# Warm-up, head-wise values and turned blocks in an attention-then-GEGLU kernel on one core

## The chip, the core and the metric

The kernel runs on one core of a Trainium2 chip. The core has five engines that run side by side, each through its own queue in order: TensorE (PE, matmuls and transposes into PSUM; its weight loads are shown as PEld), VectorE (DVE), ScalarE (ACT), GpSimd (POOL) and SyncE (SP). DMAs are issued from the queues of SP and POOL and run on 16 shared DMA engines. [...] The metric is the device time of one execution in microseconds (us), lower is better.

## The reference

Attention over 8 batches of 8 heads, with 16 "beacon" keys and values ahead of 576 causal ones, and then a gated feed-forward block over the 4608 tokens:

```python
B, H, S, D = q.shape                       # 8, 8, 576, 64; Nb = 16
k_all = concat([beacon_k, k], axis=2)      # 592 keys
v_all = concat([beacon_v, v], axis=2)
scores = q @ k_all.T / sqrt(D)
scores = where(causal, -1e9, scores)       # beacons are seen by every query
a = softmax(scores)
x = (a @ v_all).transpose(0, 2, 1, 3).reshape(B * S, H * D)   # 4608 x 512
g = x @ w_gate                             # 512 x 1536
out = (gelu(g) * (x @ w_val)) @ w_out      # 1536 x 512, result 4608 x 512 float32
```

The kernel computes it in bfloat16 with float32 sums.

## The kernel before

**Attention of one batch.** Heads are handled in pairs (`NPAIR` = 4, index m; `hi` is the head within the pair). Queries and keys lie turned in `qkT`. Scores of a pair come out turned (keys on partitions), in four chunks of columns (`CHUNKS`); `scores` (L246) does the matmuls of two or three chunks into one of the three two-bank buffers of the pool `psum_s`, lets ScalarE take the exp into `exp_ring`, and from batch 1 on lets POOL zero the masked part with `affine_select` (`masks`, L292). In batch 0 the mask is added on TensorE from two small constants, `eye` and `neg`. `attend` (L313) multiplies the exps with the values, which carry a column of ones, so that the row sums come along; `normalize` (L341) on VectorE takes the reciprocal and multiplies, into `y_sb`. For a pair both heads lie in one two-bank buffer `x_ps` of `psum_s`; batch 0's first pair alone uses the two one-bank pools `psum_t` and `psum_o`.

**Turning y.** The feed-forward block wants x with the features on partitions, in `xT_sb`. `turn` (L359) does five transposes on TensorE into PSUM and `put` (L378) copies them out; `turn_dma` (L367) does it with DMA transposes from SP. In batches 1 to 7 pairs 0 and 1 go by DMA (three each), pairs 2 and 3 by TensorE.

**Feed-forward.** Tokens go in nine chunks of 512. `gv_mms` (L390) does gate and value matmuls of one slot fi of 128 features (twelve slots, four k-chunks kk, one for each head pair), ScalarE the gelu, VectorE the product into `hT_sb`. `out_mms` (L452) does the output matmuls: 48 for a chunk, four tiles ti of twelve, whose sums lie by turns in `psum_t` and `psum_o`; `out_store` (L442) copies a finished tile and stores it from SP.

**Order.** The order on every engine is that of the program (`keep`). The main loop (L558) runs over the batches b; in it `o(n)` puts the next n output matmuls of chunk b - 1 between the attention steps of batch b, so that TensorE has work while ScalarE takes exps. After the attention come the gate and value matmuls of chunk b. Once the masks of batch b are done, POOL issues the loads of v for batch b + 1 and of q and k for b + 2 (batches 1 to 6 have at least one of these). SP first stores and turns y, then issues ten DMA transposes of the next batch's q and k (`transpose_dma`, L235). Chunk b needs columns 512b to 512b + 511 of `xT_sb`, batch b writes columns 576b to 576b + 575; so chunk 7 needs only the first 64 tokens of batch 7.

**The start.** Before batch 0's data are there, `warm(50)` (L230, L520) keeps TensorE busy with matmuls of the constant `idle`. Queries and keys of batches 0 and 1 are turned on TensorE from `qk` (`transpose_half`, L210; `transpose_pe`, L197). POOL makes `eye` and `neg` (L467 to L489) between its loads.

Of the kernel before, what the change touches and what calls it, by code (L numbers as in the profile page):

```python
# [7 lines left out]
P = 128  # L8
B, H, S, NB, D = 8, 8, 576, 16, 64
SK = S + NB  # L10
N_TOK = B * S
# [40 lines left out]
def kernel(  # L52
# [23 lines left out]
    psum_o = ctx.enter_context(tc.tile_pool(name="psum_o", bufs=1, space=bass.MemoryType.PSUM))  # L76

    eye = const.tile([P, 256], BF16, name="eye", tag="eye")
    nc.vector.memset(eye, 0.0)
    ident = eye[:, 64:192]  # L80
    idle = const.tile([P, P], BF16, name="idle", tag="idle")
    nc.vector.memset(idle, 0.0)
    wg_sb = const.tile([P, K_CHUNKS, D_FF], BF16, name="wg_sb", tag="wg_sb")
    wv_sb = const.tile([P, K_CHUNKS, D_FF], BF16, name="wv_sb", tag="wv_sb")
    wo_sb = const.tile([P, F_TILES, D_MODEL], BF16, name="wo_sb", tag="wo_sb")
    xT_sb = const.tile([P, NPAIR, N_TOK], BF16, name="xT_sb", tag="xT_sb")

    exp_ring = ring.tile([P, NPAIR, 2, EXP_W + P - Q_N[4]], BF16, name="expT", tag="expT")
    nc.vector.memset(exp_ring[:, :, :, EXP_W:], 0.0)
# [13 lines left out]
    nc.vector.memset(qkT[:, :, 1, SK:640], 0.0)  # L103

    neg = const.tile([P, 256], BF16, name="neg", tag="neg")
    nc.vector.memset(neg, 0.0)

    def dma(out_ap, in_ap):
        keep(nc.gpsimd.dma_start(out=out_ap, in_=in_ap))  # L112
# [62 lines left out]
    def mm(out_ap, lhsT, rhs, start, stop, **kw):  # L175
        keep(nc.tensor.matmul(out_ap, lhsT, rhs, start=start, stop=stop, **kw))  # L176
# [33 lines left out]
    def transpose_half(b, m, w, by_act=False):  # L210
        pool, tag = ((psum_o, "o"), (psum_t, "t"))[w]
        t_ps = pool.tile([P, 1024], BF16, name="t_ps", tag=tag)
        tr_part(b, m, w, t_ps)
        out_ap = qkT[:, m, w, NB:SK].rearrange("p (t r) -> p t r", r=6)
        in_ap = t_ps[:, 0:S].rearrange("p (r t) -> p t r", r=6)
        if by_act:
            act(out_ap, in_ap, ACT.Copy)
        else:
            keep(nc.vector.tensor_copy(out_ap, in_ap))  # L219
        return t_ps  # L220
# [9 lines left out]
    def warm(n):  # L230
        w_ps = psum_s.tile([P, 2, 512], FP32, name="w_ps", tag="s")
        for j in range(n):
            mm(w_ps[:, 0, 0:D], idle, idle[:, 0:D], True, True)

    def transpose_dma(b):  # L235
        q_sb, k_sb = q_ring[b % NRING], k_ring[b % NRING]
# [73 lines left out]

    x_of = {}

    def attend(b, m, where="s"):  # L313
        i = b * NPAIR + m
        if where == "ot":
            x_ps = (
                psum_t.tile([P, 512], FP32, name="xt_ps", tag="t"),
                psum_o.tile([P, 512], FP32, name="xo_ps", tag="o"),
            )
            x_of[i] = [(x_ps[hi].rearrange("p (b c) -> p b c", b=1), hi, hi + 1) for hi in range(2)]  # L320
        else:
            x = psum_s.tile([P, 2, 512], FP32, name="x_ps", tag="s")
            x_ps = (x[:, 0, :], x[:, 1, :])
            x_of[i] = [(x, 0, 2)]
        expT, v_sb = exp_ring[:, m, :, :], v_ring[b % NRING]
        for j in range(5):
            for hi in range(2):
                for t in range(j + 1):
                    e0 = EXP_OFF[t] + S_LO[j] - S_LO[t]
                    mm(  # L330
                        x_ps[hi][:, j * DV : (j + 1) * DV],
                        expT[0 : KROWS[t], hi, e0 : e0 + P],
                        v_sb[0 : KROWS[t], t, 2 * m + hi, 0:DV],
                        t == 0,
                        t == j,
                        skip_group_check=True,
                    )

    y_of = {}

    def normalize(b, m):  # L341
        i = b * NPAIR + m
        r_sb = npool.tile([P, 2, 5, 1], FP32, name="r_sb", tag="r_sb")
        y_sb = npool.tile([P, 5, 2, D], BF16, name="y_sb", tag="y_sb")
        y_of[i] = y_sb
        for x_ps, h0, h1 in x_of.pop(i):
            x = x_ps[:, :, 0 : 5 * DV].rearrange("p b (j d) -> p b j d", d=DV)
            r = r_sb[:, h0:h1, :, :]
            keep(nc.vector.reciprocal(r, x[:, :, :, D:DV]))  # L349
            keep(  # L350
                nc.vector.tensor_tensor(  # L351
                    out=y_sb[:, :, h0:h1, :].rearrange("p j b d -> p b j d"),
                    in0=x[:, :, :, 0:D],
                    in1=r.to_broadcast([P, h1 - h0, 5, D]),
                    op=ALU.mult,
                )
            )
# [9 lines left out]
    def turn_dma(b, m):  # L367
        y_sb = y_of.pop(b * NPAIR + m)
        n0 = b * S
        for n, j0, j1, q0 in ((S_LO[1], 0, 1, 0), (P, 1, 4, S_LO[1]), (Q_N[4], 4, 5, S_LO[4])):  # L370
            keep(
                nc.sync.dma_start_transpose(
                    out=xT_sb[:, m, n0 + q0 : n0 + q0 + n * (j1 - j0)].rearrange("p (j n) -> p j n", n=n),
                    in_=y_sb[0:n, j0:j1, :, :].rearrange("p j e d -> p (j e d)"),
                )
            )
# [13 lines left out]
    def gv_mms(ci, fi, *kks, split=False, last=False):  # L390
        if (ci, fi) not in gv_of:
            if split:
                gv_of[ci, fi] = (
                    psum_t.tile([P, CH], FP32, name="g_ps", tag="t"),
                    psum_s.tile([P, 2, CH], FP32, name="v_ps", tag="s")[:, 0, :],
                )
            else:
                gv_ps = psum_s.tile([P, 2, CH], FP32, name="gv_ps", tag="s")
                gv_of[ci, fi] = (gv_ps[:, 0, :], gv_ps[:, 1, :])
        n0 = ci * CH  # L400

        def part(w):
            for kk in kks:
                mm(
                    gv_of[ci, fi][w],
                    (wg_sb, wv_sb)[w][:, kk, fi * P : (fi + 1) * P],
                    xT_sb[:, kk, n0 : n0 + CH],
                    kk == 0,
                    kk == K_CHUNKS - 1,
                    skip_group_check=True,  # L410
                )
# [40 lines left out]
    def out_mms(ci, u0, u1):  # L452
        for u in range(u0, u1):
# [8 lines left out]

    kb_sb = opool.tile([NB, H, D], FP32, name="kb_sb", tag="o_sb")
    keep(nc.sync.dma_start(out=kb_sb, in_=beacon_k[0].rearrange("h t d -> t h d")))
    load_qk6(0, 0, 2)
    load_qk6(0, 2, 4, (1,))
    keep(  # L467
# [8 lines left out]
        )  # L476
    )
    load_qk6(0, 2, 4, (0,))
    keep(
        nc.gpsimd.affine_select(  # L480
            out=neg,
            in_=neg,
            pattern=[[1, 256]],
            compare_op=ALU.is_ge,
            fill=MASKED,
            base=-64,
            channel_multiplier=-1,
        )
    )  # L489
    load_qk6(0, 4, 6)  # L490
    load_qk6(0, 6, H)
    load_v(0)
    load_gate_val(0, 2)
    load_gate_val(2, 4)
    load_gate_val(4, 8)
# [13 lines left out]

    ahead(5)  # L510

    def av(b, m, where="s"):
        attend(b, m, where)
        normalize(b, m)

    def c(*parts):
        scores(0, *parts)

    keep(nc.scalar.preload_act_table_set(SET_EXP))
    warm(50)  # L520
    keep(nc.vector.tensor_copy(qk6[0][1], kb_sb))
    transpose_both(0, 0)
    c((0, 0))
    c((0, 2))
# [10 lines left out]
    c((2, 1))  # L535
    c((3, 0))
    c((3, 2))
    c((2, 3), (3, 3))
    av(0, 0, "ot")
    c((3, 1))  # L540
    av(0, 1)
    av(0, 2)
    turn(0, 0)
    put(0, 0, by_act=True)
# [13 lines left out]
    for b in range(B):  # L558
# [6 lines left out]
        if b:  # L565
# [2 lines left out]
            scores(b, (0, 0))  # L568
            scores(b, (0, 2))
            scores(b, (0, 1))  # L570
            if b == 1:
                transpose_pe(1, 3)
            ahead(2)
            o(9)
            scores(b, (0, 3), (1, 3))
            scores(b, (1, 0))
            scores(b, (1, 2))
            ahead(2)
            o(5)
# [82 lines left out]
```

## Time and profile before

| | |
|---|---|
| median of 8 runs | 372.0 us (371.04 to 372.75) |
| the profiled execution | 372.75 us; span on the core 370.7 us |
| TensorE busy | 358.9 us, 97% of the span |
| ScalarE, VectorE, GpSimd busy | 188.4, 149.6, 160.3 us |
| DMA | 38.33 MB, mean 103 GB/s |

The span runs from the first to the last instruction; the 2.05 us between it and the execution's time lie around it. Instructions are shown with their start in us from the span's beginning, their duration, engine, line of the kernel, operation, out<-in and how many are merged in the row; in brackets is the idle time of the engine before them and what ended it. [...] five output matmuls that begin at 290.99 are followed by other work at 292.08, 0.216 us each. "DMA to landing" is the time from a DMA's issue to its data's arrival, and "PSUM bank" or "buffer" below always means one that an engine still reads when TensorE wants to write it.

### The profile page before, as it was taken

How to read it: one execution, taken by the hardware profiler on the slowest of the kernel's cores; microseconds unless marked ns; L12 is line 12 of the kernel's file. 1: busy time of each engine (PE TensorE's matmuls, PEld its weight loads, DVE VectorE, ACT ScalarE, POOL GpSimd, SP SyncE). 2: the span in 40 equal slices, each digit the busy share in tenths (PEclk: the TensorE clock that was granted, in tenths of full speed). 3: DMA queues.
4: the chain of work that ended last, by engine and by line, in shares of the span. 5: the costliest groups of instructions: out<-in, count | busy, mean ns of one | idle time of the engine just before them, and what ended most of it. 6: DMA issues, size and time to landing. Idle time of an engine off the chain costs nothing.

```text
span 370.7 us, 7504 instructions
## 1 busy us (share of the span) xinstructions
PE 358.9 (97%) x3022; PEld 184.0 (50%) x3072; DVE 149.6 (40%) x254; ACT 188.4 (51%) x243; POOL 160.3 (43%) x284
## 2 busy tenths in 40 slices
PE   7999999999999999999999999999999999999996
PEld 6674545544554455444554455445544554444443
DVE  2454543543344425433444335333444254334332
ACT  3773477436753486338833774357534863331210
POOL 8934377942387146743495149524800430000000
PEclk9999999999999999999999999999999999999999
DMA  7999999999169943999299929991691030000112
GB/s 102 168 198 205 195 117 122 141 124 142 46 123 147 136 53 91 129 152 102 62 143 153 90 73 112 149 135 47 122 148 31 33 94 21 0 2 28 57 39 105
DMA packets 149858, 38.33 MB, mean 103 GB/s; under 512 B 136384, under 2 KB 145344, under 8 KB 149824
## 3 DMA queue, kind: packets, MB, share of 16 engines
q0 software_dynamic: 104992, 19.13, 70.6%
q1 hardware_dynamic: 44832, 18.73, 27.6%
q8 instruction: 24, 0.39, 0.5%
q14 instruction: 10, 0.08, 0.1%
HBM read 38.27 MB, written 9.44 MB: 129 GB/s over the span
## 4 chain that ended last, share of the span: by engine, by line
PE 81%; DMA 10%; POOL 2%; issue 2%; ACT 2%; SPq 1%; DVE 1%; POOLq 0%; ACTq 0%
PE gv_ps L176 36%; PE o_ps L176 24%; PE s_ps L176 8%; PE x_ps L176 7%; DMA q_sb<-in_q_dram 6%; DMA qkT<-k_sb 4%; POOL v_sb L112 2%; PE t_ps L184 2%; ACT expT L179 2%; PE y_ps L184 1%; SPq L240 1%; PE v_ps L176 1%; PE g_ps L176 1%; DMA qk<-in_k_dram 1%; DVE qkT L219 0%
## 5 line engine op out<-in xcount | busy, mean ns | idle before, releaser
L179 ACT ACTIVATE ge_sb<-gv_ps 128x512 bf16<-128x512 f32 x101 | 59.4, 597 | 132.8 <-PE gv_ps L176 132.8
L179 ACT ACTIVATE expT<-s_ps 128x960 bf16<-128x960 f32 (+3 forms) x112 | 100.0, 964 | 22.6 <-PE s_ps L176 21.6
L425 DVE TENSOR_TENSOR hT_sb<-gv_ps,ge_sb 128x512 bf16<-128x512 f32 x101 | 69.1, 691 | 104.9 <-ACT ge_sb L179 104.9
L176 PE MATMUL gv_ps<-xT_sb,wg_sb 128*128 128x512 bf16 x400 | 107.8, 379 | 0.2
L176 PE MATMUL gv_ps<-xT_sb,wv_sb 128*128 128x512 bf16 x390 | 104.1, 379 | 0.4
L176 PE MATMUL o_ps<-wo_sb,hT_sb 128*128 128x512 bf16 (+2 forms) x413 | 100.7, 373 | 2.4 <-issue 1.1
L300 POOL TENSOR_SCALAR_AFFINE_SELECT expT<-expT 128x256 bf16<-128x256 bf16 (+2 forms) x140 | 51.8, 384 | 95.4 <-ACT expT L179 94.4
L176 PEld LDWEIGHTS <-wv_sb 128*128 128x128 bf16 x432 | 42.2, 98 | 50.7
L176 PEld LDWEIGHTS <-wg_sb 128*128 128x128 bf16 x432 | 41.1, 98 | 46.7
L176 PEld LDWEIGHTS <-hT_sb 128*128 128x128 bf16 x444 | 38.9, 98 | 43.8 <-issue 6.3
L444 DVE COPY o_sb<-o_ps 128x512 f32<-128x512 f32 (+2 forms) x37 | 25.0, 676 | 43.4 <-PE o_ps L176 43.3
L176 PE MATMUL s_ps<-qkT 64*128 64x512 bf16 (+5 forms) x384 | 34.1, 291 | 2.6 <-DMA qkT<-k_sb 0.8
L112 POOL DMA_DIRECT2D v_sb<-in_v_dram x40 | 33.6, 862 | 5.9 <-DMA wv_sb<-in_moe_w_val_dram 1.9
L176 PEld LDWEIGHTS <-expT 128*128 128x128 bf16 (+1 forms) x960 | 32.5, 97 | 6.7 <-POOL expT L300 1.6
L112 POOL DMA_DIRECT2D k_sb<-in_k_dram x30 | 25.2, 841 | 20.0 <-DMA q_sb<-in_q_dram 13.2
L176 PE MATMUL x_ps<-v_sb,expT 128*128 128x65 bf16 x930 | 33.3, 194 | 0.0
L112 POOL DMA_DIRECT2D q_sb<-in_q_dram x30 | 25.4, 879 | 6.5 <-DMA wo_sb<-in_moe_w_out_dram 3.5
L351 DVE TENSOR_TENSOR y_sb<-x_ps,r_sb 128x640 bf16<-128x640 f32 x31 | 25.6, 825 | 1.1
L176 PEld LDWEIGHTS <-qkT 64*128 64x128 bf16 x384 | 14.4, 96 | 22.9 <-issue 15.5
L349 DVE RECIPROCAL r_sb<-x_ps 128x10 f32<-128x10 f32 x31 | 6.8, 221 | 36.9 <-PE x_ps L176 36.9
L384 DVE COPY xT_sb<-y_ps 128x576 bf16<-128x576 bf16 x15 | 6.9, 458 | 10.5 <-PE y_ps L184 10.5
L184 PE MATMUL t_ps<-eye,qk 96*64 96x96 bf16 x192 | 8.3, 244 | 1.3 <-ACT expT L179 0.7
(51 smaller groups left out, 127.0 us busy)
## 6 DMA issues: line engine op xcount, KB each, us to landing
out_dram<-o_sb SPq DMA_DIRECT2D x35, 256.0 KB, 2.3
v_sb<-in_v_dram POOLq DMA_DIRECT2D x24, 128.0 KB, 7.6
q_sb<-in_q_dram POOLq DMA_DIRECT2D x24, 128.0 KB, 10.8
k_sb<-in_k_dram POOLq DMA_DIRECT2D x18, 128.0 KB, 9.8
wo_sb<-in_moe_w_out_dram POOLq DMA_DIRECT2D x3, 512.0 KB, 14.1
wg_sb<-in_moe_w_gate_dram POOLq DMA_DIRECT2D x2, 512.0 KB, 11.4
wv_sb<-in_moe_w_val_dram POOLq DMA_DIRECT2D x2, 512.0 KB, 12.9
v_sb<-in_v_dram POOLq DMA_DIRECT2D x8, 112.0 KB, 4.9
```

Of the source, the lines that this page charges most:

```text
L112: keep(nc.gpsimd.dma_start(out=out_ap, in_=in_ap))
L176: keep(nc.tensor.matmul(out_ap, lhsT, rhs, start=start, stop=stop, **kw))
L179: keep(nc.scalar.activation(out_ap, in_ap, func, **kw))
L184: keep(nc.tensor.transpose(out_ap, in_ap, ident[0:n, 0:n]))
L240: nc.sync.dma_start_transpose(out=qkT[:, :, w, c + j * P : c + j * P + n], in_=src[0:n, j, :, :].rearrange("p h d -> p (h d)"),)
L300: nc.gpsimd.affine_select(out=d, in_=d, pattern=[[0, 2], [1, n]], compare_op=ALU.is_ge, fill=0.0, base=NB if t == 0 else 0, channel_multip ...
L349: keep(nc.vector.reciprocal(r, x[:, :, :, D:DV]))
L351: nc.vector.tensor_tensor(out=y_sb[:, :, h0:h1, :].rearrange("p j b d -> p b j d"), in0=x[:, :, :, 0:D], in1=r.to_broadcast([P, h1 - h0, 5 ...
L384: keep(nc.vector.tensor_copy(out_ap, y_ps[:, 0:S]))
L425: nc.vector.tensor_tensor(out=h_of[ci][:, fi, :], in0=gv_of.pop((ci, fi))[1], in1=ge_sb, op=ALU.mult)
L444: keep(nc.vector.tensor_copy(o_sb[:, ti, c0:c1], o_ps))
```

## The change

The start:
- `idle` is widened and set first, 66 warm-up matmuls take the place of 50, and eight transposes of `idle` into an unused part of the PSUM tile are put before the turn of q of batch 0's first pair.
- batch 0's beacon values come over SP's queue as float32 and are cast by VectorE, instead of over POOL's queue.
- `neg` is made on VectorE, by a running sum along the row of `eye` (started at -1) and a scaling, instead of a `memset` and a select on POOL.
- in batch 0 the score chunk ((2, 3), (3, 3)) moves behind the values of pair 0, and (3, 1) behind those of pair 1.

The loop:
- in batch 1, five output matmuls stand before the TensorE turn of pair 3's q and k, four after it.
- pairs 0 and 1 of batches 1 to 7 take their values one head at a time (`av_head`), each into a one-bank tile, pair 0 in `psum_t` and pair 1 in `psum_o`, with scores or output matmuls between the heads.
- pair 2 is turned by DMA instead of by TensorE and a copy. All DMA turns use two transposes for a pair: the last block is taken as a full one, whose 48 extra columns lie in the next batch's place (`xT_sb` is made wider for the last batch).
- output matmuls are put elsewhere: 30 instead of 40 before the last scores, and 18 (6, 7, 5) instead of 8 (6, 2) after them; pair 3 is turned between the 7 and the 5.
- the k-chunks of the first two feature slots come in the order 0, 3, 1, 2, both slots in turn; before it was 0, 1, 2 of slot 0, then 0, 1, 2 of slot 1, then 3 of each, with the turn of pair 3 in between.

```diff
-    idle = const.tile([P, P], BF16, name="idle", tag="idle")
-    xT_sb = const.tile([P, NPAIR, N_TOK], BF16, name="xT_sb", tag="xT_sb")
+    idle = const.tile([P, 256], BF16, name="idle", tag="idle")
+    xT_sb = const.tile([P, NPAIR, N_TOK + P - Q_N[4]], BF16, name="xT_sb", tag="xT_sb")
...
         t_ps = pool.tile([P, 1024], BF16, name="t_ps", tag=tag)
+        for _ in range(8 if by_act else 0):
+            tr(t_ps[0:D, 640:768], idle[:, 0:D])
         tr_part(b, m, w, t_ps)
...
+    def av(b, m):
+        x = psum_s.tile([P, 2, 512], FP32, name="x_ps", tag="s")
+        for hi in range(2):
+            attend(b, m, hi, x[:, hi, :])
+        normalize(b, m, x, 0, 2)
+
+    def av_head(b, m, hi, pool, tag):
+        x = pool.tile([P, 1, 512], FP32, name="x_ps", tag=tag)
+        attend(b, m, hi, x[:, 0, :])
+        normalize(b, m, x, hi, hi + 1)
...
-        for n, j0, j1, q0 in ((S_LO[1], 0, 1, 0), (P, 1, 4, S_LO[1]), (Q_N[4], 4, 5, S_LO[4])):
+        for n, j0, j1, q0 in ((S_LO[1], 0, 1, 0), (P, 1, 5, S_LO[1])):
...
+    vb_sb = opool.tile([NB, H, D], FP32, name="vb_sb", tag="o_sb")
+    keep(nc.sync.dma_start(out=vb_sb, in_=beacon_v[0].rearrange("h t d -> t h d")))
...
-    load_v(0)
+    for load in key_loads(v, beacon_v, v_ring[0][:, :, :, 0:D], 0)[1:]:
+        load()
...
-    warm(50)
+    warm(66)
     keep(nc.vector.tensor_copy(qk6[0][1], kb_sb))
+    keep(nc.vector.tensor_copy(v_ring[0][0:NB, 0, :, 0:D], vb_sb))
+    keep(nc.vector.tensor_tensor_scan(neg, eye, idle, -1.0, ALU.add, ALU.add))
+    keep(nc.vector.tensor_scalar_mul(neg, neg, -MASKED))
...
+    av_head(0, 0, 0, psum_t, "t")
+    av_head(0, 0, 1, psum_o, "o")
     c((2, 3), (3, 3))
-    av(0, 0, "ot")
+    av(0, 1)
     c((3, 1))
-    av(0, 1)
     av(0, 2)
...
+            o(5)
             if b == 1:
                 transpose_pe(1, 3)
             ahead(2)
-            o(9)
+            o(4)
             scores(b, (0, 3), (1, 3))
             scores(b, (1, 0))
             scores(b, (1, 2))
             ahead(2)
-            o(5)
-            av(b, 0)
-            turn_dma(b, 0)
-            o(4)
+            o(6)
+            av_head(b, 0, 0, psum_t, "t")
             scores(b, (1, 1))
             scores(b, (2, 0))
             scores(b, (2, 2))
             ahead(2)
+            o(1)
+            av_head(b, 0, 1, psum_t, "t")
+            turn_dma(b, 0)
             o(5)
-            av(b, 1)
-            turn_dma(b, 1)
-            o(4)
             scores(b, (2, 1))
             scores(b, (2, 3), (3, 3))
             scores(b, (3, 0))
-            o(9)
+            av_head(b, 1, 0, psum_o, "o")
+            o(5)
+            av_head(b, 1, 1, psum_o, "o")
+            turn_dma(b, 1)
             scores(b, (3, 1))
             scores(b, (3, 2))
             av(b, 2)
+            turn_dma(b, 2)
             o(6)
-            turn(b, 2)
-            put(b, 2)
-            o(2)
             av(b, 3)
-            keep(nc.scalar.preload_act_table_set(SET_GELU))
-            gv_mms(b, 0, 0, 1, 2)
-            gv_mms(b, 1, 0)
+            o(7)
             turn(b, 3)
             put(b, 3)
-            gv_mms(b, 1, 1, 2)
-            gv_mms(b, 0, 3, last=True)
-            gv_mms(b, 1, 3, last=True)
+            o(5)
+            keep(nc.scalar.preload_act_table_set(SET_GELU))
+            for kk in (0, 3, 1, 2):
+                for fi in range(2):
+                    gv_mms(b, fi, kk, last=kk == 2)
```

More of the change, by code (lines that the diff above doesn't have):

```diff
@@ L78 @@
     eye = const.tile([P, 256], BF16, name="eye", tag="eye")
+    idle = const.tile([P, 256], BF16, name="idle", tag="idle")
+    nc.vector.memset(idle, 0.0)
     nc.vector.memset(eye, 0.0)
     ident = eye[:, 64:192]
-    idle = const.tile([P, P], BF16, name="idle", tag="idle")
-    nc.vector.memset(idle, 0.0)
     wg_sb = const.tile([P, K_CHUNKS, D_FF], BF16, name="wg_sb", tag="wg_sb")
@@ L105 @@
     neg = const.tile([P, 256], BF16, name="neg", tag="neg")
-    nc.vector.memset(neg, 0.0)
     def dma(out_ap, in_ap):
@@ L232, in warm @@
         for j in range(n):
-            mm(w_ps[:, 0, 0:D], idle, idle[:, 0:D], True, True)
+            mm(w_ps[:, 0, 0:D], idle[:, 0:P], idle[:, 0:D], True, True)
     def transpose_dma(b):
@@ L311, with attend @@
     x_of = {}
[L313 to L324, printed above, removed]
+    def attend(b, m, hi, x_ps):
@@ L325, in attend @@
         expT, v_sb = exp_ring[:, m, :, :], v_ring[b % NRING]
         for j in range(5):
[L327 to L337, printed above, removed]
+            for t in range(j + 1):
+                e0 = EXP_OFF[t] + S_LO[j] - S_LO[t]
+                mm(
+                    x_ps[:, j * DV : (j + 1) * DV],
+                    expT[0 : KROWS[t], hi, e0 : e0 + P],
+                    v_sb[0 : KROWS[t], t, 2 * m + hi, 0:DV],
+                    t == 0,
+                    t == j,
+                    skip_group_check=True,
+                )
@@ L339, with normalize @@
     y_of = {}
-    def normalize(b, m):
+    def normalize(b, m, x_ps, h0, h1):
         i = b * NPAIR + m
+        if h0 == 0:
+            y_of[i] = npool.tile([P, 5, 2, D], BF16, name="y_sb", tag="y_sb")
         r_sb = npool.tile([P, 2, 5, 1], FP32, name="r_sb", tag="r_sb")
[L344 to L356, printed above, removed]
-            )
+        x = x_ps[:, :, 0 : 5 * DV].rearrange("p b (j d) -> p b j d", d=DV)
+        r = r_sb[:, h0:h1, :, :]
+        keep(nc.vector.reciprocal(r, x[:, :, :, D:DV]))
+        keep(
+            nc.vector.tensor_tensor(
+                out=y_of[i][:, :, h0:h1, :].rearrange("p j b d -> p b j d"),
+                in0=x[:, :, :, 0:D],
+                in1=r.to_broadcast([P, h1 - h0, 5, D]),
+                op=ALU.mult,
+            )
+        )
@@ L408, in part @@
                     kk == 0,
-                    kk == K_CHUNKS - 1,
+                    last and kk == kks[-1],
                     skip_group_check=True,
@@ L478 @@
     load_qk6(0, 2, 4, (0,))
[L479 to L489, printed above, removed]
     load_qk6(0, 4, 6)
     load_qk6(0, 6, H)
-    load_v(0)
+    for load in key_loads(v, beacon_v, v_ring[0][:, :, :, 0:D], 0)[1:]:
+        load()
     load_gate_val(0, 2)
@@ L510 @@
     ahead(5)
-    def av(b, m, where="s"):
-        attend(b, m, where)
-        normalize(b, m)
     def c(*parts):
```

## The prediction

> **What bounds the kernel now.** I read the page's first and fourth parts, then the windows by batch, the timelines of the start and of one late batch, and the tile views of the DMA transposes. All times are of the profiled execution.
>
> ```profile
> PE 358.9 (97%) x3022; PEld 184.0 (50%) x3072; DVE 149.6 (40%) x254; ACT 188.4 (51%) x243; POOL 160.3 (43%) x284
> ...
> PE 81%; DMA 10%; POOL 2%; issue 2%; ACT 2%; SPq 1%; DVE 1%; POOLq 0%; ACTq 0%
> ```
>
> TensorE is busy nearly always and is 81% of the chain of waits. Only three things can help: fewer TensorE instructions, a faster TensorE, fewer of its few gaps. The windows, one batch each (window, length, PE busy, clock, DMA share, GB/s), show how small the gaps are:
>
> ```profile
> 88.87:128.94 40.07, 39.12 (x318) 1.00 1.22 114
> 128.94:168.43 39.49, 39.06 (x318) 1.00 1.30 109
> 168.43:208.02 39.59, 38.84 (x317) 1.00 1.18 115
> 208.02:247.32 39.30, 38.87 (x317) 1.00 1.19 112
> ```
>
> A batch without gaps takes 39.30. With the first batch of the loop (47.00 to 87.15: 40.15), the batches' excess over 39.30 is 0.85 + 0.77 + 0.19 + 0.29 = 2.1 us. Two of its causes, from the timelines of PE (start, duration, what, idle before):
>
> ```profile
> 50.61 0.70 PE L184 MATMUL t_ps<-eye,qk 96*64 96x96 bf16 x24 [0.71 <-ACT expT L179]
> ...
> 91.11 0.21 PE L176 MATMUL s_ps<-qkT 64*128 64x80 bf16 x2 [0.52 <-DMA qkT<-k_sb]
> ```
>
> The first is a PSUM buffer that an exp still holds, the second the last transpose of the next batch's keys. The start is different:
>
> ```profile
> 4.59 0.69 PE L184 MATMUL t_ps<-eye,qk 96*64 96x96 bf16 x12 [0.54 <-DMA qk<-in_k_dram]
> ...
> 6.83 0.61 PE L176 MATMUL s_ps<-qkT 64*128 64x512 bf16 x2 [0.74 <-ACT qkT L179]
> ...
> 15.06 0.69 PE L184 MATMUL t_ps<-eye,qk 96*64 96x96 bf16 x12
> ...
> 37.02 0.70 PE L184 MATMUL t_ps<-eye,qk 96*64 96x96 bf16 x24
> ```
>
> 12 transposes take as long at 15.06 as 24 at 37.02: until about 16 us TensorE runs at half speed, though the page's clock row shows 9 everywhere. The 50 warm-up matmuls (1.20 to 4.05) are followed by 0.54 idle, the first scores by 0.74.
>
> [...] neither 2.85 us of warm-up nor the broken stretch after it released it, the unbroken one from 10.46 did. [...] a transpose alone lands 2.4 us after its issue, beside the loads 6 to 10. [...] No scan is in this trace.
>
> **The change, part by part.**
>
> *Start.* 66 warm-up matmuls at 2.69/50 = 0.054 us end at 1.1 + 3.55 = 4.65, where the keys have landed (4.59). Eight transposes of idle data fill the time before q's transposes: at half speed 128 columns cost 12/9 of 96 columns' 0.057, some 0.08 to 0.11 each, 0.85 in all. The unbroken stretch becomes 1.1 to 7.0, 5.9 us[...]. If the clock rises at 5 to 7 us, ScalarE sets the pace instead: first exp about 7.8 (7.61 now, the fillers delay it), 14 exps of about 0.93 less overlap, one gap of 0.6 for pair 1's turned keys: the last ends at 20.6 instead of 16.86 + 5.18 = 22.04. Values, turns and fills behind it then end about 1.65 earlier (pair 3's turn at about 23.8 instead of 25.43). Bounds: -2.2 to +0.9, the latter when the clock stays low and the fillers only delay. Weights do not bind: wv's columns for the fifth slot land at 28.1 and are wanted at 32.6 now. I take -1.65.
>
> *Mask seed and beacon values.* GpSimd loses the neg select (0.44) and one DMA issue (0.58), so later loads are issued earlier. VectorE gains a cast of 16x512 (0.48, the row of kb), a scan and a scaling. [...] Started at 4.0 after the eye, they end by 4.9, before VectorE's key copy (now 5.44). Cost 0 (bound +0.5, if the second beacon transfer lands late).
>
> *Batch 1.* Five output matmuls (1.08) before its turn cover the 0.71: -0.7.
>
> *Turn of pair 2.* It leaves TensorE (303.18 to 303.44 and a gap, 0.30 a batch) and becomes two DMA transposes; pairs 0 and 1 go from three to two each, so SP issues six either way.
>
> *Values one head at a time.* A head is 15 matmuls, 0.455; its bank is freed by one reciprocal and one product:
>
> ```profile
> 20.14 0.20 DVE L349 RECIPROCAL r_sb<-xt_ps 128x5 f32<-128x5 f32 x1 [2.74 <-PE xt_ps L176]
> ...
> 20.37 0.49 DVE L351 TENSOR_TENSOR y_sb<-xt_ps,r_sb 128x320 bf16<-128x320 f32 x1
> ```
>
> That is about 1.0 us after its last matmul. I laid batch 6 (first output matmul 286.47 = 0) out anew, with its timeline's durations: output matmuls of 0.216, score groups of 0.74, 0.79, 0.73, 0.71 and 0.51, each with 0.1 before it. First group 0.96 to 1.70, nine output matmuls, second group 3.73 to 4.53, six, head 0 to 6.29, third group 6.39 to 7.19, one, head 1 to 7.88, five to 9.06, fourth group 9.16 to 9.96, head, five, head to 11.98, fifth group 12.08 to 12.59, pair 2 to 13.5, six to 14.8, pair 3 to 15.75, seven to 17.25, turn to 17.55, five to 18.65, four times four gate/value matmuls to 22.1 (22.04 now). Waits are in it. The third tile of outputs wants bank t 0.89 after head 1 ends: waits 0.1. Scores now come closer together, and with three buffers the last of the third group waits 0.07, of the fourth 0.09. Sum of waits 0.26, against 0.30 saved: -0.02 a batch, -0.15 over seven. Bounds -0.3 to +0.3 each.
>
> *The third pair's DMA.* In that layout the scores of (3,1), (3,2) start at 12.1 (13.9 now). ScalarE, hardly idle since 1.45, does their two exps from 12.5 to 14.3; the mask ends at 14.8, and there GpSimd's queue begins the next loads, as now:
>
> ```profile
> 105.76 0.41 POOL L300 TENSOR_SCALAR_AFFINE_SELECT expT<-expT 128x256 bf16<-128x256 bf16 x1 [0.15 <-ACT expT L179]
> 106.11 0.54 POOL L112 DMA_DIRECT2D v_sb<-in_beacon_v_dram  x1
> 106.65 4.19 POOL L112 DMA_DIRECT2D v_sb<-in_v_dram  x5
> ```
>
> Loads of v thus from 15.3. SP: pair 1's y is ready at 12.9; its two transposes (1.1 and 1.25) and pair 2's first end at 16.55, so pair 2's large one is issued at 16.6, 1.3 after the loads began. TensorE needs it after 12 more output matmuls and 12 gate/value matmuls, at 21.3, that is 4.7 after issue. Alone:
>
> ```profile
> DMA to landing us min/median/max: 2.2/2.4/5.4
> ```
>
> and there is no wait. Beside the loads the nearest rows are the next batch's first transpose (same size, issued 1.6 after the loads began; 6.0 at 108.23, 6.0 to 7.8 in the six loaded batches) and the store just ahead of it (1.1 after, 3.1 to 4.7). The transpose of 108.23 had that store ahead in its ring and landed 3.0 after it; mine has a small transpose ahead, which should be through. So 4.5 to 6.0; I take 4.95, a wait of 0.25 in batches 1 to 6: +1.5. Batch 7 has no loads.
>
> *The next batch's transposes* queue on SP behind the last store, so they start 20.1 after the batch begins (18.6 to 19.4 now), but the loads they share engines with start 1.7 to 2.5 earlier; they should land by about 40.2, wanted at 40.7. The stalls at 91 and 170 go with the rest of the excess: 2.1 - 0.7 - 0.2 kept = -1.2.
>
> **Sum.** 372.75 (the profiled execution; span 370.7 and 2.05 around it) - 1.65 - 0.7 - 0.15 - 1.2 + 1.5 = 370.55. The median of the runs, 372.0, lies 0.75 under the profiled one, which released its clock late; a start that releases early no longer has that spread, so the sum stands as it is: 370.6, 0.4% under the median.
>
> **Rivals.**
>
> *A, slower: the third pair's transpose is late.* It lands like the qkT ones, store or no store, 5.8 after issue, and TensorE waits 1.1 in six batches: 370.55 + 5.1 = 375.7. For it: every transpose within 2 us of a load's start took 6 or more. Against: each had the store ahead. It decides from a wait of 0.5 a batch, where 2.95 us of savings are used up. At 7.8 after issue it would be 3 us a batch, above 386.
>
> *B: the clock stays low* in the new stretch[...]. Then the fillers cost 0.5 to 0.9 and the start saves nothing: about 372.9. For it: 8.05 to 10.3 was busy too, and released nothing.
>
> *C: one-bank buffers* cost 0.3 a batch more (each wait followed by an exposed weight load of 0.1): 372.7.
>
> *D: no wait for the transposes at all:* 369.0.
>
> **How the numbers follow.** Forecast 0.42, A 0.22, B 0.18, C 0.10, D 0.08. About 0.2% (0.75 us) is what a measurement of this kernel can tell from no change. Below 371.25: most of the forecast (0.36), D and a little of B and C (0.03): 0.47. Above 372.75: A, and half of B and C: 0.34. Between: 0.19. The range 368.6 to 376.0 leaves out D's deeper end and A's upper half. The forecast's own range is 369.3 to 371.8.
>
> **What would show it.** Right: 12 transposes in 0.35 us before 10 us; the last exp of batch 0 near 20.6; no gap at batch 1's turn; fill matmuls of the third k-chunk start within 0.5 us of the second's end. Wrong: a gap of about 1 us there, put down to a DMA of y_sb (A); 0.69 for 12 transposes still at 13 us (B); gaps at the head matmuls or the third output tile (C). A batch window much above 39.3 from batch 2 on makes the forecast wrong.

## The result and the profile after

The changed kernel takes 383.66 us (median of 11 runs, 380.44 to 387.77) against 372.45 before: a ratio of 1.027, interval 1.025 to 1.030. Three of the eleven runs (387.4 to 387.8) count as slow, and the ratio leaves them out. The kernel is slower, where 370.6 was forecast. The profiled execution took 381.64, span 379.8.

The page's first and fourth parts for the changed kernel:

```profile
PE 358.0 (94%) x3012; PEld 184.2 (49%) x3061; DVE 152.4 (40%) x277; ACT 188.2 (50%) x243; POOL 159.1 (42%) x282
...
PE 79%; DMA 13%; SPq 3%; DVE 2%; issue 1%; POOL 0%; ACT 0%
```

TensorE has as much to do as before in a longer span: 94% instead of 97%. The new time is idle time. The waits of TensorE's matmuls (who waited <- for what: total us, times, longest) name it:

```profile
PE gv_ps L172 <- DMA xT_sb<-y_sb: 11.0, 7, 2.8
...
PE s_ps L172 <- DMA qkT<-q_sb: 0.6, 1, 0.6
```

The windows of batches 1 to 6, each from its first output matmul to that of the next batch (window, length, busy time of PE, PEld, DVE, ACT, POOL, clock, DMA share, GB/s), show how unequal the batches have become:

```profile
45.94:87.89 41.95, 39.94 (x338) 19.96 (x342) 17.67 (x32) 22.12 (x29) 28.66 (x47) 1.00 1.78 146
87.89:128.66 40.77, 39.07 (x313) 19.65 (x317) 16.26 (x29) 22.13 (x29) 20.96 (x37) 1.00 1.17 109
128.66:171.08 42.42, 39.14 (x312) 19.59 (x317) 16.27 (x29) 22.14 (x29) 20.98 (x37) 1.00 1.16 112
171.08:213.74 42.66, 39.24 (x313) 19.54 (x317) 16.27 (x29) 22.13 (x29) 20.99 (x37) 1.00 1.12 108
213.74:255.15 41.41, 39.06 (x313) 19.64 (x317) 16.26 (x29) 22.13 (x29) 20.99 (x37) 1.00 1.12 110
255.15:295.69 40.54, 39.06 (x313) 19.65 (x317) 16.27 (x29) 22.13 (x29) 12.06 (x26) 1.00 0.56 84
```

A batch without gaps took 39.3 before. What follows the last of these windows takes as long as before (80.94 to the last matmul), so the loss sits in batches 1 to 6. Batch 3 shows the place. GpSimd's timeline, where the next loads begin behind the last mask, and SyncE's, where four transposes (two of pair 1, two of pair 2) stand in one row:

```profile
143.75 0.41 POOL L298 TENSOR_SCALAR_AFFINE_SELECT expT<-expT 128x256 bf16<-128x256 bf16 x1 [0.15 <-ACT expT L175]
144.10 0.53 POOL L108 DMA_DIRECT2D v_sb<-in_beacon_v_dram  x1
144.62 4.20 POOL L108 DMA_DIRECT2D v_sb<-in_v_dram  x5
```

```profile
142.25 5.01 SPq L368 DMA_TRANSPOSE xT_sb<-y_sb  x4
147.35 1.83 SPq L442 DMA_DIRECT2D out_dram<-o_sb  x2
```

and TensorE's:

```profile
150.30 0.38 PE L172 MATMUL gv_ps<-xT_sb,wv_sb 128*128 128x512 bf16 x1
152.94 0.39 PE L172 MATMUL gv_ps<-xT_sb,wg_sb 128*128 128x512 bf16 x1 [2.26 <-DMA xT_sb<-y_sb]
```

The large transpose of pair 2, the last of SyncE's four, is issued at 146.00 and lands at 152.90. The last of TensorE's twelve gate and value matmuls that can do without it begins at 150.30, so the next could begin at 150.52, 0.22 later; it has to wait until 152.94. Each batch issues six transposes of y; the table follows pair 2's large one ("first v load" is the first from `in_v_dram`; the landing without loads is from the second experiment):

| batch | issued after the first v load | landed after issue | same, loads held back | wait |
|---|---|---|---|---|
| 1 | 0.83 | 6.11 | 4.14 | 1.51 |
| 2 | 1.76 | 5.53 | 2.48 | 1.28 |
| 3 | 1.38 | 6.90 | 4.03 | 2.26 |
| 4 | 2.89 | 6.28 | 2.49 | 2.75 |
| 5 | 1.38 | 6.55 | 4.12 | 1.93 |
| 6 | 1.67 | 5.39 | 2.49 | 1.05 |
| 7 | no loads | 3.61 | 3.85 | 0 |

The six waits add up to 10.8. The seventh wait of the 11.0 is 0.24 in batch 4, ahead of k-chunk 1, and belongs to pair 1: its large transpose was issued there at 186.43, beside the loads as well, and landed at 191.77.

The start did what was hoped for:

```profile
4.76 0.69 PE L180 MATMUL t_ps<-eye,qk 96*64 96x96 bf16 x12
...
6.22 0.45 PE L180 MATMUL t_ps<-eye,qk 96*64 96x96 bf16 x12
```

Twelve transposes take 0.69 at 4.76 and 0.45 at 6.22, and the first batch of the loop begins at 45.94 instead of 48.15.

The runs spread over 7 us, and their length goes with the granted clock: those from 380.4 to 382.8 had 0.994 or more, those from 383.7 to 387.8 had 0.986 to 0.990. The profiled one had 1.00. This is taken up in the last experiment.

### The profile page after: what moved, and what is told of

Read it like the earlier page. It is cut to its first block, busy times and chain, and to the rows that moved or that the text cites. A ratio compares the mean times of both kernels' runs of the same rounds, so it can differ in the third digit from the quotient of the medians.

```text
span 379.8 us, 7505 instructions
## 1 busy us (share of the span) xinstructions
PE 358.0 (94%) x3012; PEld 184.2 (49%) x3061; DVE 152.4 (40%) x277; ACT 188.2 (50%) x243; POOL 159.1 (42%) x282
## 4 chain that ended last, share of the span: by engine, by line
PE 79%; DMA 13%; SPq 3%; DVE 2%; issue 1%; POOL 0%; ACT 0%
PE gv_ps L172 38%; PE o_ps L172 20%; DMA xT_sb<-y_sb 9%; PE x_ps L172 8%; PE s_ps L172 8%; DMA qkT<-q_sb 2%; DMA q_sb<-in_q_dram 2%; SPq L238 2%; PE t_ps L180 2%; PE v_ps L172 1%; PE g_ps L172 1%; DVE qkT L217 1%; PE w_ps L172 1%; SPq L368 1%; PE y_ps L180 0%
## 5 line engine op out<-in xcount | busy, mean ns | idle before, releaser
L172 PE MATMUL gv_ps<-xT_sb,wg_sb 128*128 128x512 bf16 x401 | 111.4, 380 | 11.5 <-DMA xT_sb<-y_sb 11.0
L172 PE MATMUL gv_ps<-xT_sb,wv_sb 128*128 128x512 bf16 x394 | 109.4, 379 | 0.1
L172 PEld LDWEIGHTS <-wg_sb 128*128 128x128 bf16 x432 | 42.0, 98 | 63.6 <-DMA xT_sb<-y_sb 14.5
L172 PEld LDWEIGHTS <-expT 128*128 128x128 bf16 (+1 forms) x960 | 34.0, 97 | 8.7 <-issue 2.5
L172 PE MATMUL x_ps<-v_sb,expT 128*128 128x65 bf16 (+1 forms) x960 | 37.1, 194 | 0.9 <-PE s_ps L172 0.9
L336 DVE TENSOR_TENSOR y_sb<-x_ps,r_sb 128x320 bf16<-128x320 f32 (+1 forms) x47 | 28.8, 612 | 1.6
L334 DVE RECIPROCAL r_sb<-x_ps 128x5 f32<-128x5 f32 (+1 forms) x47 | 9.6, 204 | 43.8 <-PE x_ps L172 43.8
```

Of the source, the lines that this page charges most:

```text
L336: nc.vector.tensor_tensor(out=y_of[i][:, :, h0:h1, :].rearrange("p j b d -> p b j d"), in0=x[:, :, :, 0:D], in1=r.to_broadcast([P, h1 - h0 ...
```

## The experiments

All are against the kernel before on the same chip, whose medians in these comparisons were 371.8 to 372.7; runs of different groups are best compared by their ratios. Theory A: the loss is TensorE's wait for pair 2's block, and the block is late because its transposes share the DMA engines with the loads.

**Pair 2 back on TensorE.**

```diff
-            turn_dma(b, 2)
             o(6)
+            turn(b, 2, psum_o, "o")
+            put(b, 2)
```

> The changed kernel with pair 2 turned on TensorE (after the six output matmuls, into the bank of the odd output tiles) and copied by VectorE, as pair 3 is. Theory A (the whole loss is TensorE's wait for the third pair's DMA transposes: 11.0 us on the matmuls plus about 0.15 for each of the refills): the wait is gone, seven turns of 0.30 come back, 381.6 - 11.7 + 2.1 = 372.0, within 0.3% of the kernel before. Rival H (the values one head at a time and the new places of the output matmuls cost some us of their own): it stays at 374 or above.

Measured: 371.94, ratio 0.9985 (0.9968 to 1.0001). The DMA wait is gone and so is the loss. A batch takes 39.67, against 39.39 in the fourth run (the start and batch 1's turn alone), which has the old values and turns. So with pair 2 on TensorE the head-wise values and the new places of the output matmuls cost 0.28 a batch, 2 us in all, and not the further microseconds of rival H.

**The loads wait for pair 2's block.**

```diff
                 if b and b + 1 < B:
+                    keep(nc.gpsimd.tensor_copy(landed, xT_sb[0:1, 2, b * S + S - 1 : b * S + S]))
                     load_v(b + 1)
```

> The changed kernel, where GpSimd first copies one element of the third pair's turned block, so that the next loads of v, q and k cannot start before that block has landed. Theory A1 (the block lands late because it shares the DMA engines with the loads): it lands 2.4 to 3.5 us after its issue instead of 5.4 to 6.9, no wait is left of the 11 us, and the time is 369.5 to 371; what may be late next are the transposes of the next batch's q and k, up to 0.6 a batch. Rival A2 (it lands late because three pairs' transposes stand one behind the other in SP's ring): it still lands over 5 us after its issue and the time stays near 381.

Measured: 369.95, ratio 0.9929 (0.9898 to 0.9959). GpSimd's timeline in batch 2, and the landing of all transposes of y (minimum, median, maximum; the median was 3.5):

```profile
106.58 0.18 POOL L607 COPY landed<-xT_sb 1x1 bf16<-1x1 bf16 x1 [5.24 <-DMA xT_sb<-y_sb]
107.06 0.53 POOL L109 DMA_DIRECT2D v_sb<-in_beacon_v_dram  x1 [0.31 <-issue]
107.59 4.21 POOL L109 DMA_DIRECT2D v_sb<-in_v_dram  x5
```

```profile
DMA to landing us min/median/max: 2.2/2.5/5.8
```

No matmul waits for y any more. The order on SyncE is the same, so three pairs in one ring are not the cause (A2 falls); the loads in flight are. How they delay it inside the DMA engines is shown by no run here. In the table above they add 2.0 to 2.9 in the odd batches and 2.9 to 3.8 in the even ones. What is late next is, as expected, the next batch's keys:

```profile
128.26 0.21 PE L173 MATMUL s_ps<-qkT 64*128 64x80 bf16 x2 [0.72 <-DMA qkT<-k_sb]
```

**More cover.**

```diff
-                for fi in range(2):
+                for fi in range(3):
                     gv_mms(b, fi, kk, last=kk == 2)
         for fi in range(F_TILES):
-            if fi >= 2:
+            if fi >= (3 if b else 2):
```

> The changed kernel with three feature slots instead of two interleaved by k-chunk: 18 instead of 12 gate and value matmuls ahead of the first use of the third pair's block, 1.3 us more cover. If the waits are those of the block alone, 1.5, 1.3, 2.3, 3.0, 1.9, 1.1 become 0.2, 0, 1.0, 1.7, 0.6, 0: about 7.5 saved, 374. If its gelu and product come so close together that the next slots wait for a buffer, up to 0.5 of it is lost in each of seven batches: 377.

Measured: 380.36, ratio 1.022 (1.017 to 1.026). The waits for the block are 0 in batch 1 and then 0.62, 1.07, 0.88, 1.08 and 0.87, 4.5 in all; but a wait for a buffer is new, 0.90 in batch 1 and 0.55 in each later one, 4.2 in all. Batch 3:

```profile
152.07 0.39 PE L172 MATMUL gv_ps<-xT_sb,wg_sb 128*128 128x512 bf16 x1 [1.07 <-DMA xT_sb<-y_sb]
...
154.09 1.02 PE L172 MATMUL gv_ps<-xT_sb,wg_sb 128*128 128x512 bf16 x4 [0.55 <-DVE hT_sb L421]
```

All three buffers finish at once, and the fourth slot waits for the first slot's gelu and product. Of the 6.5 gained on the block, 4.2 are paid back. Both expected times, 374 and 377, were missed.

**The start and batch 1's turn alone.** The loop is that of the kernel before, but for

```diff
+            o(5)
             if b == 1:
                 transpose_pe(1, 3)
             ahead(2)
-            o(9)
+            o(4)
```

> The kernel before with the change's start and its five output matmuls ahead of batch 1's turn alone; values, turns and fills as before. The change's trace has its first batch of the loop begin 2.2 earlier, and the 0.71 at the turn is gone: 372.5 - 2.2 - 0.7 = 369.6, a ratio of 0.992. If the early start is only lent (later waits for weights or keys take it back), 371 to 372.

Measured: 369.79, ratio 0.9929 (0.9906 to 0.9952). The loop begins at 45.51 instead of 48.15 and the later batches without a stall take 39.39 (39.30 before; where the 0.09 come from is open), so the gain is kept.

**A second wait, for the loads of q and k.**

```diff
+                    keep(nc.gpsimd.tensor_copy(landed, qkT[0:1, 0, 1, SK - 1 : SK]))
                     load_qk(b + 2)
```

with the transposes of q and k issued ahead of it in the program.

> As the run in which the loads wait for the third pair's block, and the loads of q and k also wait until the last of the ten transposes of the next batch's q and k has landed. If what is left there (0.72 and 0.21 before scores, put down to the last keys' transpose) is the same sharing of the DMA engines, these two go: 0.9 less, 369.1. If those transposes are late because they stand behind one another, nothing changes: 370.0.

Measured: 372.37, ratio 1.0021 (1.0003 to 1.0039). Neither. GpSimd's timeline from batch 2 into batch 3, which begins at 126.36, and TensorE's there:

```profile
122.80 0.18 POOL L612 COPY landed<-qkT 1x1 bf16<-1x1 bf16 x1 [10.38 <-DMA qkT<-k_sb]
123.31 4.20 POOL L109 DMA_DIRECT2D q_sb<-in_q_dram  x5 [0.34 <-issue]
127.46 0.58 POOL L109 DMA_DIRECT2D k_sb<-in_beacon_k_dram  x1
127.98 4.24 POOL L109 DMA_DIRECT2D k_sb<-in_k_dram  x5
132.15 2.84 POOL L299 TENSOR_SCALAR_AFFINE_SELECT expT<-expT 128x224 bf16<-128x224 bf16 x8
```

```profile
132.69 1.00 PE L173 MATMUL x_ps<-v_sb,expT 128*128 128x65 bf16 x9 [0.33 <-POOL expT L299]
```

The transposes did land early, at 122.7 (128.2 in the run with one wait), so the loads were the cause of those stalls too. But the eleven loads, 9 us of issuing, now stand ahead of batch 3's masks in GpSimd's queue, and the values wait for the masks. What is queued behind a held-back load had been left out of the expectation.

**Pair 2 by DMA, values by pairs.** Pairs 0 and 1 take their values as in the kernel before, loads are held back, and the tail is the change's without its last five output matmuls, which have gone ahead of the scores. Against the loop of the kernel before:

```diff
             scores(b, (3, 0))
-            o(9)
+            o(4)
             scores(b, (3, 1))
             scores(b, (3, 2))
             av(b, 2)
+            turn_dma(b, 2)
             o(6)
-            turn(b, 2)
-            put(b, 2)
-            o(2)
             av(b, 3)
+            o(7)
             turn(b, 3)
...
```

> The change without its values one head at a time: pairs 0 and 1 take their values together as in the kernel before, pair 2 goes by DMA, and the loads wait for it. The batch of the kernel with the start and batch 1's turn alone is 39.39; without pair 2's turn on TensorE it is 0.30 shorter, 39.1, seven times 0.3 less than 369.8: 367.7 if no transpose is late, 368.6 with the two stalls of the next batch's keys. If scores now wait for one of the three two-bank buffers (four output matmuls stand where nine stood), a wait of 0.3 or more shows in each batch and the time is 370 or more.

Measured: 375.89, ratio 1.0115 (1.0092 to 1.0137). The rival held, in every batch (here batch 2):

```profile
100.91 0.37 PE L173 MATMUL s_ps<-qkT 64*128 64x464 bf16 x2 [0.20 <-ACT expT L176]
101.82 1.07 PE L173 MATMUL x_ps<-v_sb,expT 128*128 128x65 bf16 x30 [0.54 <-ACT expT L176]
```

With five output matmuls moved behind the last scores, ScalarE's exps end too late. In the change, the head-wise values fill that place, and with the loads held back no such wait is left there: the two parts belong together. Even with the loads held back, batch 5 waits 0.50 for pair 2's block here, which landed after 4.67 and had five output matmuls less to hide behind. The same with the second wait:

> The run before with the second wait for the loads of q and k as well: 367.7 if the two stalls were the sharing, otherwise as the run before.

Measured: 380.56, ratio 1.024 (1.0215 to 1.0262); both stalls in every batch, and from batch 2 on the masks late as well.

**The start taken apart.** From the run with the start and batch 1's turn alone, without the eight transposes of idle data:

```diff
-        for _ in range(8 if by_act else 0):
-            tr(t_ps[0:D, 640:768], idle[:, 0:D])
```

> The start and batch 1's turn alone, without the eight transposes of idle data ahead of q's turn. If TensorE must be busy without a break for the clock to rise early, the break of about 0.5 comes back at 5 us, 12 transposes still take 0.69 at 13 us, and the 2.2 us of the start go: 372. If the longer warm-up alone is enough, the time stays at 369.8 or falls by some 0.2.

and then with 50 warm-up matmuls as well:

```diff
-    warm(66)
+    warm(50)
```

> The start and batch 1's turn alone, with 50 warm-up matmuls as in the kernel before and without the transposes of idle data. Theory W (an unbroken stretch from the first warm-up matmul on releases the clock early): the break of 0.5 before the first turn is back, the clock rises near 13 to 16 us, and the gain of the start goes: 371.7. Rival V (the gain comes from the moved score chunks and the mask seed, not from the clock): within 0.5 of the runs with 66, 369.8 to 370.8.

Measured: 370.80, ratio 0.9966 (0.9951 to 0.9982), and 371.57, ratio 0.9988 (0.9972 to 1.0004). TensorE without the idle transposes:

```profile
4.76 0.69 PE L180 MATMUL t_ps<-eye,qk 96*64 96x96 bf16 x12
...
7.55 0.45 PE L180 MATMUL t_ps<-eye,qk 96*64 96x96 bf16 x12
```

and with 50 warm-ups:

```profile
4.69 0.69 PE L180 MATMUL t_ps<-eye,qk 96*64 96x96 bf16 x12 [0.72 <-DMA qk<-in_k_dram]
...
8.17 0.69 PE L180 MATMUL t_ps<-eye,qk 96*64 96x96 bf16 x12
...
15.82 0.45 PE L180 MATMUL t_ps<-eye,qk 96*64 96x96 bf16 x12
```

Without the idle transposes no break came back, since 66 warm-ups last until the keys are there; only the second run brings the break. With its gap of 0.72 twelve transposes still take 0.69 at 8.17, and 0.45 by 15.82; without a gap they take 0.45 by 7.55. In these traces theory W holds, and rival V falls. In the profiled executions the loop begins at 48.15 before, at 47.51 with 50 warm-ups, at 45.65 with 66 and at 45.51 with the idle transposes too. That would give the sixteen warm-ups 1.86 and the idle transposes 0.14, but a profile is one execution: the one without idle transposes took 369.25, 1.55 less than the median of its runs, so it shows one of the early releases. By the ratios the sixteen warm-ups bring 0.8 (0.9988 to 0.9966, with intervals that overlap) and the idle transposes 1.4 (0.9966 to 0.9929). So most of what the start gains is the clock's early rise, and the idle transposes seem to make it come in more of the runs (9 of 14 took 370.2 or less with them, 5 of 22 without); how the gain divides is known only roughly.

**The large transpose first.**

```diff
-        for n, j0, j1, q0 in ((S_LO[1], 0, 1, 0), (P, 1, 5, S_LO[1])):
+        parts = ((S_LO[1], 0, 1, 0), (P, 1, 5, S_LO[1]))
+        for n, j0, j1, q0 in parts[::-1] if m == 2 else parts:
```

> The changed kernel with the two transposes of pair 2 issued the other way round, the large one first; loads as in the change. In its trace the large one is issued 0.8 to 2.9 us after the first load of v began and lands 5.4 to 6.9 us later. If each microsecond of load ahead of it costs landing time, issuing it 1.2 earlier brings its landing 2 to 3 us forward, the small one lands 3.5 after its own issue at the old place of the large one, and 1 to 2.3 us of each wait go: 11.0 falls to 2 to 4, 373 to 375. If a transpose that meets the loads at all lands 5.5 to 7 after its issue wherever it stands, only the 1.2 of earlier issue are gained, at most: 375 to 377.

Measured: 382.71, ratio 1.030 (1.024 to 1.035). In batch 5 the large one, issued 0.36 after the first load of v, landed 6.8 later, and the small one behind it 7.2 later; over batches 1 to 6 the large ones took 3.6 to 6.8 (5.4 to 6.9 in the change) and the small ones 4.9 to 7.2. So a transpose that meets the loads is late in either place. The waits add up to 7.8 instead of 11.0, and the profiled execution took 379.90 instead of 381.64, but by the ratio the kernel is no faster. Both expected times were missed, and part of the reason is in the trace. TensorE after the wait of that batch:

```profile
233.35 0.61 PE L172 MATMUL gv_ps<-xT_sb,wg_sb 128*128 128x512 bf16 x1 [2.78 <-DMA xT_sb<-y_sb]
...
234.60 0.63 PE L172 MATMUL gv_ps<-xT_sb,wv_sb 128*128 128x512 bf16 x1
235.02 1.78 PE L172 MATMUL gv_ps<-xT_sb,wg_sb 128*128 128x512 bf16 x4
236.64 1.03 PE L172 MATMUL gv_ps<-xT_sb,wv_sb 128*128 128x512 bf16 x4
```

A gate matmul takes 0.61 instead of 0.38, and starts follow each other after some 0.42 instead of 0.22: the clock had fallen to half, for 3.4 us, as the windows of the wait and of what followed show too (the granted clock is the third figure from the end):

```profile
230.60:233.10 2.50, 0.00 (x0) 0.00 (x0) 0.00 (x0) 0.00 (x0) 1.67 (x3) 1.00 1.30 121
233.10:236.50 3.40, 3.15 (x8) 1.19 (x9) 1.29 (x2) 1.19 (x2) 2.00 (x3) 0.50 1.71 216
```

That batch took 44.02, 1.9 more than 39.3 and its wait.

**Transposes of q and k before the last stores.** With the loads held back for pair 2's block:

```diff
             turn_dma(b, 2)
+            if b + 1 < B:
+                transpose_dma(b + 1)
...
-                if 2 <= b + 1 < B:
-                    transpose_dma(b + 1)
```

> As the run in which the loads wait for the third pair's block, with the ten transposes of the next batch's q and k issued from SP ahead of the last two stores of the batch. They start 1.1 to 1.7 us earlier and meet fewer loads; the two stalls left there (0.72 and 0.21) go: 0.7 to 0.9 less than 369.95, 369.1. If the stores, which now wait 12 us on SP, keep a tile that the next output tile or the last transposes need, 370 or more.

Measured: 368.95, ratio 0.9926 (0.9899 to 0.9953). Its windows of batches 2 to 4:

```profile
85.78:125.09 39.31, 39.31 (x318) 19.74 (x317) 16.26 (x29) 22.12 (x29) 21.20 (x38) 1.00 1.18 112
125.09:164.40 39.31, 39.31 (x318) 19.74 (x317) 16.27 (x29) 22.13 (x29) 21.20 (x38) 1.00 1.15 124
164.40:203.72 39.32, 39.32 (x319) 19.72 (x318) 16.27 (x29) 22.13 (x29) 21.20 (x38) 1.00 1.18 106
```

TensorE is never idle in them. This version beats both kernels, the one before by 0.7%, and it is the change plus one copy of one element and one call moved.

**Work inside the wait.** In the changed kernel, batches 1 to 6:

```diff
+                if kk == 2 and b < B - 1:
+                    f_ps = psum_o.tile([P, CH], FP32, name="f_ps", tag="o")
+                    for _ in range(5):
+                        mm(f_ps, idle[:, 0:P], wo_sb[:, 0, :], True, True)
```

> The changed kernel, with five matmuls of constant data (1.08 us) into a free bank just ahead of the second k-chunk that waits, in batches 1 to 6. They lie inside a wait of 1.05 to 2.8 and should cost nothing in a run whose clock stays high: the profiled time stays at 381 to 382. Theory K (a wait of about 2.8 us lets the clock fall to half for some 3 us afterwards, as one batch of the run with the large transpose first shows: 0.61 to 0.63 for a gate matmul after a wait of 2.78, 0.38 else): the waits without work are now under 2, no run has a granted clock under 0.995, the runs lie within 2 of each other and their median falls from 383.7 to 381.5. Rival: the clock falls for another reason (the start, or load), and runs at 385 to 388 still occur.

Measured: 379.61 (five runs, 378.1 to 380.46), ratio 1.0185 (1.0159 to 1.0211), all with a granted clock of 0.995 or more; the profiled one took 380.46. Batch 4 of the profiled run:

```profile
191.67 1.24 PE L172 MATMUL f_ps<-wo_sb,idle 128*128 128x512 bf16 x5
193.83 0.39 PE L172 MATMUL gv_ps<-xT_sb,wg_sb 128*128 128x512 bf16 x1 [0.92 <-DMA xT_sb<-y_sb]
```

By the ratios (1.0185, and 1.027 for the change) five idle matmuls a batch made the kernel 3 us faster, and no run came near 385. Not all of that is the clock. Among runs with a granted clock of 0.994 or more the change's median is 381.64 (five of its eleven runs), 2.0 above; and the profiled run, expected at 381 to 382, is shorter at the same clock, where its blocks landed somewhat earlier (5.3 to 6.1): 3.0 of waits and 6.5 of idle matmuls stand for 11.0 of waits. What remains, that no run fell to 0.99 or below where six of the change's eleven did, speaks for theory K together with the half-speed stretch above. It isn't settled: five runs are few, and in the kernel before, runs with a granted clock of 0.99 are no longer than the rest.

## Why the prediction was wrong, by its own steps

**The start: -1.65 forecast, -2.21 measured.** The clock rose in the unbroken stretch (by 6.22, as the transposes above show), the first exp came at 7.92 (7.8 forecast), the last exp of batch 0 ended at 20.61 (20.6), pair 3's turn came at 23.23 (23.8). Rival B did not happen in the profile. That the stretch would be long enough was the author's estimate: the trace before shows one release from half speed, near 16 us in the stretch from 10.46, and not how short a stretch suffices. One support did not hold: the spread of 1.7 that an early release was to remove is that of eight runs; the 32 runs beside the result spread over 3.5, and the 14 of the run with the start and batch 1's turn alone over 3.8.

**The mask seed: 0 forecast, 0 measured.** VectorE's timeline:

```profile
3.94 0.69 DVE L507 TENSOR_TENSOR_SCAN neg<-eye,idle 128x256 bf16<-128x256 bf16 x1 [0.28 <-POOL eye L466]
4.67 0.23 DVE L508 TENSOR_SCALAR neg<-neg 128x256 bf16<-128x256 bf16 x1
```

The scan took 0.69 and the scaling 0.23. The end by 4.9 was the author's estimate, as the trace before has no scan; they are done at 4.9, before the key copy at 5.61.

**Batch 1: -0.7 forecast, -0.45 measured** (40.72 before, 40.27 with the loads held back). The stall before the turn went, but a new one of 0.3 stands behind it:

```profile
48.81 0.70 PE L180 MATMUL t_ps<-eye,qk 96*64 96x96 bf16 x24
...
50.52 1.06 PE L172 MATMUL s_ps<-qkT 64*128 64x208 bf16 x8
51.51 1.47 PE L172 MATMUL o_ps<-wo_sb,hT_sb 128*128 128x512 bf16 x6
```

These scores take 0.99, and 0.70 before, where nine output matmuls instead of four stood between turn and scores. VectorE's copies out of the turned block's buffer run until 51.15, and the trace puts a wait of 0.12 within the scores, at 51.21, down to the last of them; no run shows more of it.

**Values by heads and pair 2's turn: -0.02 a batch forecast, 0.00 measured.** Where no transfer is late, a batch takes 39.31, as a gapless one before. Where pair 2 stays on TensorE and the saving of 0.30 is missing, the rest costs 0.28 (39.67 against 39.39), about the 0.26 of waits that the layout had; rival C's further 0.3 did not come.

**Stalls elsewhere: -1.2 forecast, some -0.45 measured.** Batches 2 and 4 lost 0.59 and 0.46 before; in the change batch 3 loses 0.60 to the next batch's q. Those transposes were forecast to land 0.5 before they are wanted, which is less than their landings vary.

**The third pair's DMA: +1.5 forecast, +12.1 measured. This is the step that failed.** The cause, the loads beside the block (landed after 5.39 to 6.90 with them, 2.48 to 4.14 with them held back), and the place were right, and the need nearly so: outside batch 4 the block was wanted 4.1 to 4.5 after its issue (4.7 forecast), and the loads had begun 0.8 to 1.8 before (1.3 forecast). The term that was mis-sized is the landing: "4.5 to 6.0; I take 4.95". It measured 5.4 to 6.9, 6.13 in the mean. Landing less need was forecast at 0.25 and came to 1.9 in the mean; of the 1.7 between, 1.2 are the landing and 0.5 the need (4.2 in the mean, 3.4 in batch 4). The nearest rows that the prediction had, 6.0 to 7.8 for the next batch's first transpose, were set aside with an argument; taken as they stood, they cover four of the six landings and lie above the other two. The argument for the low value, that a store ahead in the ring had delayed the transposes of the kernel before, falls with the runs: whether it was first or second in its pair made little difference (3.6 to 6.8 and 5.4 to 6.9), and without loads, with the same ring, it landed after 2.5 to 4.1. Rival A was the case, with 5.8 as its landing and 1.1 as its wait; the waits were 1.05 to 2.75. Two things were added: in batch 4 the issue itself came 1.2 later against the loads than in batches 2 and 6, behind an issue on SyncE that took 2.4 instead of 1.1, and pair 1's block came late there too (0.24); and each wait costs some 0.2 more than its idle time, most of it the matmul before it (shown with 0.38, where the next could begin after 0.22). The 12.1 is the sum of the six windows, 249.75 less its other stall of 0.60, against 237.99 less 0.93 with the loads held back. Then -2.21 - 0.45 - 0.45 + 12.1 = +9.0, and the spans differ by 9.1.

The chances did not reflect the leverage. With no slack left, every 0.1 of landing costs 0.6, so the upper end of the landing's own range, 6.0, is 7.8 us of waits where 1.5 were counted; the range given ended at 376.0, which is a landing of 5.85. (A and half of B and C add up to 0.36, not to 0.34; nothing hangs on it.)

**The rest, 2.0 between the profiled execution and the median,** was in no term: the waits seem to cost clock as well, which the last experiment makes likely and does not settle.

## What to carry to other kernels

A DMA that moves work off the busiest engine is bought with slack: read its landing time in the company that it will keep (here up to 6.90), not alone (2.48 to 4.14 with the loads held back), and multiply the uncertainty by how often the wait stands in the loop. If the transfers beside it have slack of their own, hold these back with one element's copy that reads what must land first, and then look at what is queued behind the held-back instruction. Test the parts of a change apart: here the start and batch 1's turn gave 0.7% at once, while the part that cost 12 us brings no more than 0.1 us a batch even when mended.

## What the hardware showed that was not expected

- A single wait of 2.78 us on TensorE was followed by 3.4 us at half clock, a loss of 1.9 us (the run with the large transpose first). A wait of 2.75 in batch 4 of the change's profiled execution went by without it: the 3.4 us that followed, from 195.60, had a granted clock of 1.00. What decides between the two is not shown; a wait of this length is a risk.
- A large transpose of y can land late with no load in flight too: pair 2's after 4.14, 2.48, 4.03, 2.49, 4.12, 2.49 and 3.85 in batches 1 to 7 of the run with the loads held back, and in the same pattern in the run with the transposes of q and k moved. Batches that follow each other write to places that lie 1152 bytes apart, but the place alone is not the reason: in the run with values by pairs, whose transposes write to the same columns, the large one landed after 2.48 in batches 1, 3 and 7 as well and was late in batch 5 alone (4.67). What delays it is open.
- Work that computes nothing paid for itself: without the sixteen further warm-up matmuls (0.85 us) and the eight idle transposes a gap of 0.72 stood before the first turn, twelve transposes still took 0.69 at 8.17, and the time was 371.57 (ratio 0.9988); with both it was 369.79 (0.9929).
